# Scores of two heads as products of 64 rows in turns, in a fused attention and two feed-forward stages

## The chip, the cores and the metric

The kernel runs on one core of one Trainium2 chip. The metric is the device time of one execution in microseconds, as the median of several executions. TensorE multiplies and transposes, VectorE (DVE), ScalarE (ACT) and GpSimd (POOL) work element by element, SyncE (SP) issues the DMAs. Products land in PSUM, of which the kernel uses eight banks; everything else is kept in SBUF.

## What is computed

Three stages one after another, all in float32, for a batch of 4 sequences of 448 positions: a causal attention of 12 heads of width 64; a feed-forward of width 1024 with a convolution over three positions and a gate; and a mixture of 4 experts, each of which is a causal attention of one head of width 64, weighted by a gate that takes the best two of four.

```
scores = scale * np.matmul(q, k.transpose(0, 1, 3, 2))
scores = np.where(mask, -1000000000.0, scores)
attn = softmax(scores)
x = np.matmul(attn, v)
...
h = np.maximum(x @ w_in, 0.0)
conv_out = sum of conv_w[k] * h shifted by k - 1
x = h * sigmoid(conv_out) @ w_out
...
for e in range(E):
    q, k, v = x @ wq[e], x @ wk[e], x @ wv[e]
    a = causal softmax of scale * (q @ k.transpose(0, 2, 1))
    out += gate weight of e * (a @ v @ wo[e])
```

## The kernel before

**Planner.** The kernel does not issue its work as it is written. Each step is given to a planner (class `Plan`, `P.op`) with its cost on each engine that may do it, the buffers that it reads (`r`) and writes (`w`), and a function that issues it. `run` (L291) works out a rank for each step, lays the steps on the engines in simulated time (`schedule`, L330), moves the ranks by the table `SHIFTS` of seeded noise in given windows, and then issues all steps in order of their planned start. So the order on every queue, and which of ScalarE, VectorE and GpSimd does a conversion, follow from the cost figures and from `SHIFTS`; at run time each engine works through its own queue in that order and waits on semaphores. TensorE's steps are named "T", VectorE's "V", ScalarE's "A", GpSimd's "G", DMAs "D". A step is planned as one piece: nothing else is put between the instructions that its function issues.

**Split products.** Precision is kept by splitting a float32 operand into a high part, rounded to the type that TensorE takes in one pass (`high`, L595), and a low part, the difference (`low`, L606). A product a*b is summed in PSUM as high*high + low*high + high*low, three passes (`products`, L888). A head has only 64 rows to contract, half of TensorE's 128, so the scores (L615 to L688) use stacked operands: for one head, `qs` holds q's high part on the head's own 64 rows and q's low part on the other 64; `kh` holds k's high part on both halves; `kl` (tile `z`) holds k's low part on the own half and zeros on the other. Two products of 128 rows then make the three terms:

```
nc.tensor.matmul(bank(c), qs()[:, rows], kh()[:, kc(c)], start=True, stop=False)
nc.tensor.matmul(bank(c), qs()[:, rows], kl()[:, kc(c)], start=False, stop=True)
```

**Score blocks.** The 448 query positions are cut into four row blocks `c` (`Q0`, `QN`), whose causal widths are 64, 192, 320 and 448 columns. Blocks 3 and 0 of a head share the PSUM bank `sx`, blocks 2 and 1 the bank `sy`. For each block there are two products (L653, L654), a masked minimum that VectorE reads out of the bank (L660), and an exponential with its sum on ScalarE (L664). Then come reciprocals and a scaling of the weights (L674 to L688), transposes on TensorE (L691), the products with v (`weigh`, L741) and the splitting of the result (`gather`, L765). There is one `sx` and one `sy`, so the next head's blocks wait until VectorE has read the bank.

**Operands of the scores.** For 21 of the 24 attention pairs of heads `prepare` (L776) loads q and k of two heads as [128 rows, 2, 448], head 0 on rows 0 to 63 and head 1 on rows 64 to 127 (tile `full`), and makes the stacked operands: per head a conversion of 64 rows by 896 columns (q and k high), a copy of k high to the other half on ScalarE ("k again"), q low to the other half, and k low into `z`. The first three pairs (`WHOLE_QK`) skip the splitting: their scores are full float32 products of 128 rows with a block-diagonal k (L651). In the expert stage `project` (L1051) computes q and k of two experts at once into a bank `pf` and makes the same stacked operands per expert: two high parts of q and two of k on ScalarE, two low parts of q, two copies of k and the low parts of k on VectorE.

**Stages.** The attention of batch 0 runs first, beside the conversion of the feed-forward's weights; the attention of batch b + 1 is laid beside the feed-forward of batch b; the expert stage, with the projections of two batches ahead, follows from about 380 us on. In `full`, only one load of q and k (`raw`) is held at a time.

## Time and profile before

| what | us |
|---|---|
| median of 3 runs | 626.16 |
| lowest and highest run | 621.04, 626.28 |
| the profiled execution's own time | 625.61 |
| its span, first to last instruction | 623.8 |
| mean granted TensorE clock, share of full speed | 0.986 |

The profile is one execution, taken by the hardware profiler. Its views give busy time per engine, stretches of the span, groups of instructions by line and shape, the timeline, and the chain of work that ended last. PE is TensorE's products, PEld its weight loads, which run beside the products. Matmuls are pipelined and their ends are modelled: a product's own duration holds the time that it takes to pass through the array, so the distance between starts, not the duration, says what a product costs in a run of products. Idle time of an engine that is not the bottleneck costs nothing.

### The profile page before, as it was taken

How to read it: one execution, taken by the hardware profiler on the slowest of the kernel's cores; microseconds unless marked ns; L12 is line 12 of the kernel's file. 1: busy time of each engine (PE TensorE's matmuls, PEld its weight loads, DVE VectorE, ACT ScalarE, POOL GpSimd, SP SyncE). 2: the span in 40 equal slices, each digit the busy share in tenths (PEclk: the TensorE clock that was granted, in tenths of full speed). 3: DMA queues.
4: the chain of work that ended last, by engine and by line, in shares of the span. 5: the costliest groups of instructions: out<-in, count | busy, mean ns of one | idle time of the engine just before them, and what ended most of it. 6: DMA issues, size and time to landing. Idle time of an engine off the chain costs nothing.

```text
span 623.8 us, 10496 instructions
## 1 busy us (share of the span) xinstructions
PE 589.8 (95%) x3348; PEld 522.1 (84%) x3348; DVE 512.0 (82%) x1391; ACT 445.4 (71%) x1102; POOL 215.5 (35%) x241
## 2 busy tenths in 40 slices
PE   7999999989899999998999999979999899999997
PEld 3787788878788988887989987868999798999976
DVE  6999999998999979899987985982164979966982
ACT  5999798889779759999866994451142657745773
POOL 4765223545543016876201631641001202210320
PEclk9999999999799999998999999999999999999999
DMA  7645614374873065561007639616824040020123
GB/s 217 180 123 165 183 62 157 122 251 173 272 258 81 0 202 193 203 222 43 2 17 241 197 109 392 193 47 245 310 51 150 30 149 30 2 89 0 46 85 137
DMA packets 50455, 87.75 MB, mean 141 GB/s; under 512 B 21856, under 2 KB 31456, under 8 KB 50400
## 3 DMA queue, kind: packets, MB, share of 16 engines
q1 hardware_dynamic: 50400, 87.09, 42.9%
q8 instruction: 26, 0.43, 0.3%
q14 instruction: 29, 0.24, 0.1%
HBM read 64.26 MB, written 22.81 MB: 140 GB/s over the span
## 4 chain that ended last, share of the span: by engine, by line
PE 49%; DVE 25%; ACT 16%; issue 5%; DMA 3%; POOL 1%; SPq 1%; ACTq 0%; DVEq 0%; POOLq 0%
PE pf L896 30%; PE t L691 5%; DVE half L921 5%; DVE pair L607 4%; ACT e L664 4%; PE po L750 4%; DMA full<-in_qk 3%; ACT pair L599 3%; DVE a L607 3%; DVE e L660 3%; DVE z L607 2%; ACT e L680 2%; PE po L736 2%; ACT a L599 2%; PE sx L654 2%
## 5 line engine op out<-in xcount | busy, mean ns | idle before, releaser
L896 PE MATMUL pf<-pair,wbig 128*128 128x448 f32 x984 | 217.7, 370 | 5.4 <-ACT hp L910 4.1
L896 PEld LDWEIGHTS pf<-pair,wbig 128*128 128x128 f32 x984 | 180.6, 188 | 23.0 <-ACT hp L910 6.0
L664 ACT ACTIVATE e<-e,stat 128x448 f32<-128x448 f32 (+3 forms) x256 | 127.5, 500 | 19.5 <-DVE stat L660 18.5
L896 PE MATMUL pf<-pair,thou 128*128 128x448 f32 x576 | 133.5, 379 | 6.0 <-DVE pair L607 4.4
L896 PEld LDWEIGHTS pf<-pair,thou 128*128 128x128 f32 x576 | 108.8, 194 | 16.2 <-DVE pair L607 5.3
L691 PE MATMUL t<-ident,e 128*128 128x128 f32 x512 | 85.0, 280 | 3.5 <-DVE a L607 1.1
L607 DVE TENSOR_TENSOR a<-t,a 64x448 fp32r<-64x448 f32 (+1 forms) x96 | 75.5, 787 | 7.7 <-ACT a L599 5.9
L599 ACT ACTIVATE pair<-pf 128x448 fp32r<-128x448 f32 (+3 forms) x64 | 30.5, 492 | 60.3 <-PE pf L896 46.8
L691 PEld LDWEIGHTS t<-ident,e 128*128 128x128 f32 x512 | 61.6, 142 | 13.9 <-DVE a L607 4.7
L599 ACT ACTIVATE a<-t 64x448 fp32r<-64x448 f32 (+1 forms) x96 | 64.3, 673 | 8.8 <-PE t L691 6.0
L750 PE MATMUL po<-a,thou 128*128 128x384 f32 (+5 forms) x336 | 64.1, 312 | 2.4 <-DVE half L762 2.1
L683 POOL TENSOR_SCALAR e<-e,stat,coef 128x448 f32<-128x448 f32 (+3 forms) x37 | 21.3, 588 | 121.5 <-DVE coef L1165 63.5
L660 DVE CUSTOM_DVE_ANT_0 e<-sy,mask 128x192 f32<-128x192 f32 (+1 forms) x128 | 51.0, 416 | 10.5 <-PE sy L654 9.8
L607 DVE TENSOR_TENSOR pair<-pf,pair 128x448 fp32r<-128x448 f32 (+1 forms) x40 | 24.8, 621 | 35.6 <-ACT pair L599 35.1
L921 DVE SCALAR_TENSOR_TENSOR half<-hp,cws,half 128x448 f32<-128x448 f32 x64 | 49.9, 796 | 4.5 <-ACT half L916 4.0
L750 PEld LDWEIGHTS po<-a,thou 128*128 128x128 f32 (+1 forms) x336 | 47.6, 177 | 6.5 <-DVE half L762 3.4
L660 DVE CUSTOM_DVE_ANT_0 e<-sx,mask 128x448 f32<-128x448 f32 (+1 forms) x128 | 51.4, 414 | 1.9 <-PE sx L654 0.7
L607 POOL TENSOR_TENSOR pair<-half,pair 128x448 fp32r<-128x448 f32 x23 | 26.8, 1167 | 71.7 <-DVE pair L601 45.6
L680 ACT ACTIVATE e<-e,stat 128x192 f32<-128x192 f32 (+3 forms) x100 | 45.5, 501 | 5.0 <-DVE stat L676 4.7
L664 ACT ACTIVATION_READ_ACCUMULATOR e<-e,stat 128x1 f32 x256 | 48.3, 189 | 0.0
L599 ACT ACTIVATE pair<-full 64x448 fp32r<-64x448 f32 (+1 forms) x62 | 43.2, 696 | 6.3 <-DMA full<-in_qk 5.2
L607 POOL TENSOR_TENSOR thou<-half,thou 128x512 fp32r<-128x512 f32 x23 | 31.8, 1389 | 40.0 <-ACT thou L599 24.2
(116 smaller groups left out, 998.5 us busy)
## 6 DMA issues: line engine op xcount, KB each, us to landing
thou<-w_scratch SPq DMA_DIRECT2D x36, 512.0 KB, 5.0
x_scratch<-pair SPq DMA_DIRECT2D x24, 448.0 KB, 4.0
pair<-x_scratch SPq DMA_DIRECT2D x24, 448.0 KB, 5.4
full<-in_w_in SPq DMA_DIRECT2D x12, 512.0 KB, 4.0
full<-in_w_out SPq DMA_DIRECT2D x12, 512.0 KB, 4.0
w_scratch<-thou SPq DMA_DIRECT2D x12, 512.0 KB, 4.4
out<-half SPq DMA_DIRECT2D x24, 224.0 KB, 1.9
half<-in_vv SPq DMA_DIRECT2D x16, 256.0 KB, 5.0
```

What stands on the lines that cost most here:

```text
L599: nc.scalar.activation(dst(), src(), AF.Copy)
L607: return lambda e: engine(e).tensor_sub(dst(), src(), f32(h()))
L654: nc.tensor.matmul(bank(c), qs()[:, rows], kl()[:, kc(c)], start=False, stop=True)
L660: nc.vector.tensor_tensor_reduce(out=ec(c), in0=blocked(bank(c)), in1=blocked(m), scale=-0.125, scalar=3.0e38, op0=OP.add, op1=OP.min, acc ...
L664: nc.scalar.activation(ec(c), ec(c), AF.Exp, bias=st[:, 0, c:c + 1], scale=-1.0, accum_out=st[:, 1, c:c + 1])
L680: nc.scalar.activation(ec(c), ec(c), AF.Copy, scale=st[:, 3, c:c + 1])
L683: engine(en).tensor_scalar(ec(c), ec(c), st[:, 3, c:c + 1], gate, op0=OP.mult, op1=OP.mult)
L691: P.op({"T": TURN}, lambda _: nc.tensor.transpose(dst(), src(), ident), r=r, w=keys, m=m)
L736: lambda _, a=a, j=j, x=col + 64 * j - q, y=col + S - q: nc.tensor.matmul(ps[:, 64 * j:S], v(PLACE[j]), a[:, x:y], start=j == 0, stop=j == ...
L750: lambda _: nc.tensor.matmul(ps[:n, q:S], v(k, m), rhs(), start=start, stop=stop),
L896: nc.tensor.matmul(out_ap(), a(), b(), start=first, stop=end), r=r, w=[(ps, 0)])
L921: return lambda _: nc.vector.scalar_tensor_tensor(cv[:, :S], hp[:, i:S + i], cws[:, fc, i:i + 1], cv[:, :S], op0=OP.mult, op1=OP.add)
```

## The change

The stacked operands go. For a pair of heads there is one tile of high parts and one of low parts, q and k of head 0 on rows 0 to 63 and of head 1 on rows 64 to 127, as the load brings them. `prepare` needs one conversion of 128 rows by 896 columns and two subtractions of 128 rows by 448 columns; `project` one high and one low part of q for both experts, and per expert the high and low part of k. `scores` takes both heads of a pair. A row block has three products per head, q high with k high, q low with k high, q high with k low, each of 64 rows, and the two heads take turns product by product: head 0 on rows 0 to 63 into its bank `sx`, head 1 on rows 64 to 127 into its bank `sy`. Each head has one bank for all of its blocks: blocks 3 and 0 first, 2 and 1 after. The twelve products of two blocks are one step, which the planner counts as 3.6 (`SIDES`) times the time of one 128-row product of each width. The whole-precision scores of the first three pairs keep their form. The tiles `z` go, and there are 20 tiles `pair` in place of 18. Operands of the same values are multiplied; the rest of the computation is unchanged. The table `SHIFTS` is another, with 26 entries in place of 37, so the planner's order is new on all engines.

```diff
+SIDES = 3.6
...
 SHIFTS = (
-    (14931, 21, 61, 0.5), (51895, 149, 159, 2), (69609, 112, 152, 0.5), (19965, 135, 175, 0.5), (49972, 65, 75,
+    (50226, 530, 540, 1), (2079, 416, 436, 2), (83136, 282, 292, 1), (43264, 499, 539, 1), (58582, 209, 229, 1),
...
-      "qk high": ("AVG", "AVG"), "k again": "A", "q low": "VG", "k low": "VG", "v high": ("V", "AG")}
+      "qk high": ("AVG", "AVG"), "qk low": "VG", "v high": ("V", "AG")}
...
-    zs = tiles("z", 2, [128, 2, S], F32R)
-    for t in zs:
-        for o in range(2):
-            nc.gpsimd.memset(f32(t[HALF[1 - o], o]), 0.0)
...
-    zk = Kind(zs)
-    pairs = Kind(tiles("pair", 18, [128, 2, S], F32R))
+    pairs = Kind(tiles("pair", 20, [128, 2, S], F32R))
...
-    def scores(qs, kh, qk_r, kl, kl_r, j, e, turns=False):
-        sb = {3: P.buf("sx"), 2: P.buf("sy")}
-        sb[0], sb[1] = sb[3], sb[2]
-        st, o = P.buf("st"), j % 2
+    def scores(qk, j, e, turns=False):
+        whole = isinstance(qk, list)
+        sbs = [{3: P.buf("sx"), 2: P.buf("sy")} for _ in range(2)]
+        if not whole:
+            sbs = [{3: sbs[0][3], 2: sbs[1][3]}, {3: sbs[0][2], 2: sbs[1][2]}]
+        for sb in sbs:
+            sb[0], sb[1] = sb[3], sb[2]
+        sts = [P.buf("st") for _ in range(2)]
...
-        def bank(c):
-            return sb[c][:, COL[c]:COL[c] + Q0[c] + QN[c]]
...
+        def bank(o, c):
+            return sbs[o][c][:, COL[c]:COL[c] + Q0[c] + QN[c]]
+        def ec(o, c):
...
-        def kc(c):
+        def kc(o, c):
...
-        for c in ORDER:
-            w = Q0[c] + QN[c]
-            rows = slice(Q0[c], Q0[c] + 128)
-            if kl is None:
-                pe = 4 * w / 2400
-            else:
-                pe = product(w) + max(product(w), 0.107)
-            def mm(_, c=c, w=w, rows=rows):
-                if kl is None:
-                    nc.tensor.matmul(bank(c), qs()[:, rows], kh()[:, :w // 64], start=True, stop=True)
-                    return
-                nc.tensor.matmul(bank(c), qs()[:, rows], kh()[:, kc(c)], start=True, stop=False)
-                nc.tensor.matmul(bank(c), qs()[:, rows], kl()[:, kc(c)], start=False, stop=True)
-            P.op({"T": pe}, mm, r=qk_r + kl_r, w=[(sb[c], c)])
-            def mx(_, c=c, w=w):
+        def weight(o, c):
+            w, st, sb = Q0[c] + QN[c], sts[o], sbs[o]
+            def mx(_):
                 m = mask[:, 448 - w:448] if c and (o or turns) else mask[:, 320:320 + w]
-                nc.vector.tensor_tensor_reduce(out=ec(c), in0=blocked(bank(c)), in1=blocked(m), scale=-0.125, scalar=3.0e38,
+                nc.vector.tensor_tensor_reduce(out=ec(o, c), in0=blocked(bank(o, c)), in1=blocked(m), scale=-0.125, scalar=3.0e38,
                                                op0=OP.add, op1=OP.min, accum_out=st[:, 0, c:c + 1])
-            def ex(_, c=c):
-                nc.scalar.activation(ec(c), ec(c), AF.Exp, bias=st[:, 0, c:c + 1], scale=-1.0,
+            def ex(_):
+                nc.scalar.activation(ec(o, c), ec(o, c), AF.Exp, bias=st[:, 0, c:c + 1], scale=-1.0,
                                      accum_out=st[:, 1, c:c + 1])
             P.op({"V": on_vector(w)}, mx, r=[(sb[c], c)], w=[(e, (o, c)), (st, ("m", c))])
             P.op({"A": on_scalar(w) + 0.23}, ex, r=[(st, ("m", c))], w=[(e, (o, c)), (st, ("s", c))])
+        if whole:
+            for o, (qs, kh, r) in enumerate(qk):
+                for c in ORDER:
+                    w = Q0[c] + QN[c]
+                    P.op({"T": 4 * w / 2400}, lambda _, o=o, c=c, w=w, qs=qs, kh=kh: nc.tensor.matmul(
+                        bank(o, c), qs()[:, Q0[c]:Q0[c] + 128], kh()[:, :w // 64], start=True, stop=True), r=r, w=[(sbs[o][c], c)])
+                    weight(o, c)
+        else:
+            q, k, r = qk
+            for two in (ORDER[:2], ORDER[2:]):
+                def mm(_, two=two):
+                    for c in two:
+                        for i, (s, t) in enumerate(((0, 0), (1, 0), (0, 1))):
+                            for o, own in enumerate(HALF):
+                                nc.tensor.matmul(bank(o, c), q(s)[own, Q0[c]:Q0[c] + 128], k(t)[own, kc(o, c)], start=i == 0, stop=i == 2)
+                P.op({"T": sum(SIDES * max(product(Q0[c] + QN[c]), 0.107) for c in two)}, mm, r=r,
+                     w=[(sbs[o][c], c) for c in two for o in range(2)])
+                for c in two:
+                    for o in range(2):
+                        weight(o, c)
+        for o, st in enumerate(sts):
+            norms(j + o, st, o, ec, e)
+    def norms(j, st, o, ec, e):
...
-        raw, z = P.buf("raw"), P.buf("z")
-        sts = [P.buf("qks") for _ in range(2)]
+        raw, hi, lo = P.buf("raw"), P.buf("qks"), P.buf("qks")
...
         if turn:
-            P.op(dma_cost(229376, 1792), load(lambda: raw[:, :S], qk[p, :, 0]), w=[(raw, 0)], hold=[z] + sts)
+            P.op(dma_cost(229376, 1792), load(lambda: raw[:, :S], qk[p, :, 0]), w=[(raw, 0)], hold=[hi, lo])
...
         else:
-            P.op(dma_cost(458752), load(both, qk[p]), w=[(raw, i) for i in range(4)], hold=[z] + sts)
-        res, src = [], [(raw, i) for i in range(4)]
-        for o in range(2):
-            own, oth, st = HALF[o], HALF[1 - o], sts[o]
-            P.op(copy_cost(2 * S, ON["qk high"][ph]), high(lambda st=st, own=own: st[own], lambda own=own: both()[own]), r=src, w=[(st, 0)])
-            P.op(copy_cost(S, ON["k again"]), high(lambda st=st, oth=oth: st[oth, 1], lambda own=own: both()[own, 1]), r=src, w=[(st, 1)])
-            P.op(two_cost(S, ON["q low"]), low(lambda st=st, oth=oth: st[oth, 0], lambda own=own: both()[own, 0], lambda st=st, own=own: st[own, 0]),
-                 r=src + [(st, 0)], w=[(st, 2)])
-            P.op(two_cost(S, ON["k low"]), low(lambda own=own, o=o: z[own, o], lambda own=own: both()[own, 1], lambda st=st, own=own: st[own, 1]),
-                 r=src + [(st, 0)], w=[(z, o)])
-            res.append((lambda st=st: st[:, 0], lambda st=st: st[:, 1], [(st, i) for i in range(3)],
-                        lambda o=o: z[:, o], [(z, o)]))
-        return res
+            P.op(dma_cost(458752), load(both, qk[p]), w=[(raw, i) for i in range(4)], hold=[hi, lo])
+        src = [(raw, i) for i in range(4)]
+        P.op(copy_cost(2 * S, ON["qk high"][ph]), high(lambda: hi[:, :, :], both), r=src, w=[(hi, 0)])
+        for i in range(2):
+            P.op(two_cost(S, ON["qk low"]), low(lambda i=i: lo[:, i], lambda i=i: both()[:, i], lambda i=i: hi[:, i]), r=src + [(hi, 0)], w=[(lo, i)])
+        return lambda s: (hi, lo)[s][:, 0], lambda s: (hi, lo)[s][:, 1], [(hi, 0), (lo, 0), (lo, 1)]
...
-        return [(lambda: qw[:, :S], lambda o=o: kb[:, :, o], [(qw, 0), (kb, o)], None, []) for o in range(2)]
+        return [(lambda: qw[:, :S], lambda o=o: kb[:, :, o], [(qw, 0), (kb, o)]) for o in range(2)]
...
-            for o in range(2):
-                scores(*ops[o], 2 * p + o, e, whole)
+            scores(ops, 2 * p, e, whole)
...
-        heads = [(P.buf("q2"), P.buf("k2")) for _ in range(2)]
-        ops = {}
+        ops = []
...
-            (q, kh), kl = heads[pr], P.buf("kl2")
+            q, kt = P.buf("q2"), P.buf("k2")
...
-                for o in range(2):
-                    own, oth = HALF[o], HALF[1 - o]
-                    src = lambda ps=ps, own=own: ps[own, :S]
-                    if isk:
+                if isk:
+                    for o, own in enumerate(HALF):
                         more = 0.0 if o else 0.06
-                        P.op({"A": on_scalar(S) + more}, turn(high, o, lambda o=o, own=own, kh=kh: kh[own, o], src), r=[(ps, 0)], w=[(kh, (o, 0))])
-                        P.op(copy_cost(S, "V"), high(lambda o=o, oth=oth, kh=kh: kh[oth, o], lambda o=o, own=own, kh=kh: f32(kh[own, o])),
-                             r=[(kh, (o, 0))], w=[(kh, (o, 1))])
-                        P.op({"V": on_vector(S) + more}, turn(low, o, lambda o=o, own=own, kl=kl: kl[own, o], src, lambda o=o, own=own, kh=kh: kh[own, o]),
-                             r=[(ps, 0), (kh, (o, 0))], w=[(kl, (o, 0))])
-                        ops[2 * pr + o] = (lambda q=q, o=o: q[:, o], lambda kh=kh, o=o: kh[:, o],
-                                           [(q, (o, 0)), (q, (o, 1)), (kh, (o, 0)), (kh, (o, 1))],
-                                           lambda kl=kl, o=o: kl[:, o], [(kl, (o, 0))])
-                    else:
-                        P.op(psum_cost(S), high(lambda o=o, own=own, q=q: q[own, o], src), r=[(ps, 0)], w=[(q, (o, 0))])
-                        P.op({"V": on_vector(S)}, low(lambda o=o, oth=oth, q=q: q[oth, o], src, lambda o=o, own=own, q=q: q[own, o]),
-                             r=[(ps, 0), (q, (o, 0))], w=[(q, (o, 1))])
+                        src = lambda ps=ps, own=own: ps[own, :S]
+                        P.op({"A": on_scalar(S) + more}, turn(high, o, lambda own=own, kt=kt: kt[own, 0], src), r=[(ps, 0)], w=[(kt, (o, 0))])
+                        P.op({"V": on_vector(S) + more}, turn(low, o, lambda own=own, kt=kt: kt[own, 1], src, lambda own=own, kt=kt: kt[own, 0]),
+                             r=[(ps, 0), (kt, (o, 0))], w=[(kt, (o, 1))])
+                else:
+                    P.op(psum_cost(S), high(lambda q=q: q[:, 0], lambda ps=ps: ps[:, :S]), r=[(ps, 0)], w=[(q, 0)])
+                    P.op({"V": on_vector(S)}, low(lambda q=q: q[:, 1], lambda ps=ps: ps[:, :S], lambda q=q: q[:, 0]), r=[(ps, 0), (q, 0)], w=[(q, 1)])
+            ops.append((lambda s, q=q: q[:, s], lambda s, kt=kt: kt[:, s], [(q, 0), (q, 1)] + [(kt, (o, s)) for o in range(2) for s in range(2)]))
...
-            for o in range(2):
-                scores(*ops[2 * pr + o], B * H + b * E + 2 * pr + o, e)
+            scores(ops[pr], B * H + b * E + 2 * pr, e)
```

On TensorE, the scores of the first pair that is not in whole precision, before: pair_112 is the stacked operand of one head, z_98 its low part of k, block_105 and po_166 belong to the product of another pair's weights with v.

```order
L653 MATMUL sy_165<-pair_112 128x320
L654 MATMUL sy_165<-z_98,pair_112 128x320
L653 MATMUL sy_165<-pair_112 128x192
L654 MATMUL sy_165<-z_98,pair_112 128x192
L736 MATMUL po_166<-half_143,block_105 128x384
L736 MATMUL po_166<-half_143,block_105 128x128
L736 MATMUL po_166<-half_144,block_105 128x320
L653 MATMUL sx_164<-pair_112 128x64
L654 MATMUL sx_164<-z_98,pair_112 128x64
L653 MATMUL sx_164<-pair_112 128x448
L654 MATMUL sx_164<-z_98,pair_112 128x448
```

After, pair_106 holds the high parts and pair_107 the low parts of both heads; this is the first of the two steps of the pair, blocks of 448 and 64 columns.

```order
L669 MATMUL sx_160<-pair_106 128x448
L669 MATMUL sy_161<-pair_106 128x448
L669 MATMUL sx_160<-pair_106,pair_107 128x448
L669 MATMUL sy_161<-pair_106,pair_107 128x448
L669 MATMUL sx_160<-pair_107,pair_106 128x448
L669 MATMUL sy_161<-pair_107,pair_106 128x448
L669 MATMUL sx_160<-pair_106 128x64
L669 MATMUL sy_161<-pair_106 128x64
L669 MATMUL sx_160<-pair_106,pair_107 128x64
L669 MATMUL sy_161<-pair_106,pair_107 128x64
L669 MATMUL sx_160<-pair_107,pair_106 128x64
L669 MATMUL sy_161<-pair_107,pair_106 128x64
```

Eight products of a head came in pieces of two to four with other work between; now twelve products stand in one piece, and every second one goes to the other bank.

On VectorE, the operands of the first such pair before: full_136 is the load of q and k.

```order
L601 CAST pair_112<-full_136 64x896
L607 TENSOR_TENSOR z_98<-full_136,pair_112 64x448
L607 TENSOR_TENSOR pair_112<-full_136,pair_112 64x448
L607 TENSOR_TENSOR pair_113<-full_136,pair_113 64x448
L607 TENSOR_TENSOR z_98<-full_136,pair_113 64x448
L660 ISA e_159,stat_82<-sy_165,mask 128x5x64
```

After, the low parts of q and k of both heads, two instructions; the conversion to the high parts stands on GpSimd.

```order
L865 SCALAR_TENSOR_TENSOR half_140<-full_134,half_140 128x512
L694 TENSOR_SCALAR e_155<-e_155,stat_83 128x64
L694 TENSOR_SCALAR e_155<-e_155,stat_83 128x7x64
L600 TENSOR_TENSOR pair_107<-full_132,pair_106 128x448 x2
L644 ISA e_156,stat_84<-sy_161,mask 128x5x64
```

Five instructions of 64 rows became two of 128 rows, later in the queue; the three on ScalarE and none on GpSimd became one on GpSimd.

On VectorE, the operands of the first four experts before: pf_145 and pf_146 are the banks of the projections.

```order
L607 TENSOR_TENSOR pair_122<-pf_145,pair_122 64x448 x2
L601 CAST pair_119<-pair_119 64x448
L607 TENSOR_TENSOR z_99<-pf_146,pair_119 64x448
L607 TENSOR_TENSOR z_99<-pf_146,pair_119 64x384
L607 TENSOR_TENSOR z_99<-pf_146,pair_119 64x64
L601 CAST pair_119<-pair_119 64x448
L607 TENSOR_TENSOR pair_116<-pf_145,pair_116 64x448 x2
L601 CAST pair_113<-pair_113 64x448
L607 TENSOR_TENSOR z_98<-pf_146,pair_113 64x384
L607 TENSOR_TENSOR z_98<-pf_146,pair_113 64x64
L607 TENSOR_TENSOR z_98<-pf_146,pair_113 64x448
L601 CAST pair_113<-pair_113 64x448
```

After, in the same place:

```order
L600 TENSOR_TENSOR pair_111<-pf_141,pair_111 128x448
L600 TENSOR_TENSOR pair_117<-pf_142,pair_117 64x384
L600 TENSOR_TENSOR pair_117<-pf_142,pair_117 64x64
L600 TENSOR_TENSOR pair_117<-pf_142,pair_117 64x448
L600 TENSOR_TENSOR pair_115<-pf_141,pair_115 128x448
L600 TENSOR_TENSOR pair_106<-pf_142,pair_106 64x384
L600 TENSOR_TENSOR pair_106<-pf_142,pair_106 64x64
L600 TENSOR_TENSOR pair_106<-pf_142,pair_106 64x448
```

A subtraction of 128 rows stands for two of 64, and the copies of k within a tile (CAST pair<-pair) are gone; the low parts of k (448, or 384 and 64 columns) stay.

## Rows read from the trace of the kernel before

**Rows 1.** The page's table of engines: busy us, share of the span, instructions.
```profile
PE 589.8 (95%) x3348; PEld 522.1 (84%) x3348; DVE 512.0 (82%) x1391; ACT 445.4 (71%) x1102; POOL 215.5 (35%) x241
```

**Rows 2.** Stretches of the span: us; each engine's busy us and instructions; clock; DMA.
```profile
40.00:220.00 180.00, 169.67 (x913) 146.98 (x912) 172.27 (x433) 154.83 (x378) 71.15 (x70) 0.97 0.50 156
...
140.00:160.00 20.00, 16.79 (x90) 14.52 (x90) 18.31 (x49) 18.43 (x47) 11.31 (x13) 0.84 0.58 202
440.00:460.00 20.00, 20.00 (x101) 18.53 (x100) 5.74 (x11) 4.38 (x9) 0.00 (x0) 1.00 0.53 189
```

**Rows 3.** The page's chain of work that ended last, by engine.
```profile
PE 49%; DVE 25%; ACT 16%; issue 5%; DMA 3%; POOL 1%; SPq 1%; ACTq 0%; DVEq 0%; POOLq 0%
```

**Rows 4.** Timeline of TensorE, one head's score products: start, us, operation.
```profile
261.99 0.38 PE L653 MATMUL sy<-pair 128*128 128x320 f32 x1 [0.73 <-DVE stat L676]
262.21 0.31 PE L654 MATMUL sy<-z,pair 128*128 128x320 f32 x1
262.36 0.36 PE L653 MATMUL sx<-pair 128*128 128x448 f32 x1
262.56 0.37 PE L654 MATMUL sx<-z,pair 128*128 128x448 f32 x1
262.77 0.25 PE L653 MATMUL sy<-pair 128*128 128x192 f32 x1
262.86 0.28 PE L654 MATMUL sy<-z,pair 128*128 128x192 f32 x1
262.97 0.22 PE L653 MATMUL sx<-pair 128*128 128x64 f32 x1
263.02 0.28 PE L654 MATMUL sx<-z,pair 128*128 128x64 f32 x1
263.13 0.46 PE L896 MATMUL pf<-pair,thou 128*128 128x448 f32 x1
```

**Rows 5.** Timeline of TensorE's weight loads in the same stretch.
```profile
262.77 0.19 PEld L654 LDWEIGHTS sy<-z,pair 128*128 128x128 f32 x1
262.88 0.19 PEld L653 LDWEIGHTS sx<-pair 128*128 128x128 f32 x1
```

**Rows 6.** Groups by line and shape: count, busy us, mean ns of one, idle before.
```profile
L660 DVE CUSTOM_DVE_ANT_0 e<-sx,mask 128x448 f32<-128x448 f32 x64 | 39.4, 616 | 1.5 <-PE sx L654 0.7 <-PE sx L651 0.3
...
L599 ACT ACTIVATE pair<-full 64x448 fp32r<-64x448 f32 x42 | 24.2, 577 | 4.7 <-DMA full<-in_qk 3.9
...
L607 DVE TENSOR_TENSOR z<-full,pair 64x448 fp32r<-64x448 f32 x28 | 19.8, 707 | 0.4
...
L599 ACT ACTIVATE pair<-full 64x896 fp32r<-64x896 f32 x20 | 18.9, 947 | 1.6 <-DMA full<-in_qk 1.3
L607 DVE TENSOR_TENSOR pair<-full,pair 64x448 fp32r<-64x448 f32 x24 | 18.9, 788 | 0.7
...
L607 DVE TENSOR_TENSOR pair<-pf,pair 128x448 fp32r<-128x448 f32 x24 | 14.8, 621 | 24.8 <-ACT pair L599 24.6
...
L601 DVE CAST pair<-half 128x448 fp32r<-128x448 f32 x25 | 11.3, 456 | 0.3
...
L607 DVE TENSOR_TENSOR pair<-pf,pair 64x448 fp32r<-64x448 f32 x16 | 10.0, 622 | 10.8 <-ACT pair L599 10.6
...
L601 DVE CAST pair<-full 64x896 fp32r<-64x896 f32 x10 | 7.0, 699 | 4.5 <-DMA full<-in_qk 3.9 <-DMA x_scratch<-pair 0.5
...
L601 DVE CAST pair<-pair 64x448 fp32r<-64x448 f32 x16 | 6.5, 404 | 8.0 <-ACT pair L599 7.7
```

**Rows 7.** Timeline of TensorE, products into 64 columns between transposes.
```profile
252.41 0.42 PE L750 MATMUL po<-a,thou 128*64 128x128 f32 x2
252.68 0.49 PE L691 MATMUL t<-ident,e 128*128 128x128 f32 x3
```

More of the change, by code (lines that the diff above doesn't have):

```diff
@@ L579, in attention_moe_moe @@
             ("wbig0", big[0], 1), ("wbig1", big[1], 1), ("xs", pairs, 8), ("g", pairs, 8), ("qks", pairs, 4),
-            ("x2s", pairs, 2), ("x2", pairs, 12), ("y", pairs, 4), ("xm", pairs, 2), ("q2", pairs, 4), ("k2", pairs, 4), ("kl2", zk, 2),
+            ("x2s", pairs, 2), ("x2", pairs, 12), ("y", pairs, 4), ("xm", pairs, 2), ("q2", pairs, 4), ("k2", pairs, 4),
             ("vs", thou, 2), ("w2", thou, 4), ("w2b", thou, 6), ("vs2", thou, 6),
@@ L583, in attention_moe_moe @@
             ("hp", Kind(hps), 2), ("st", Kind(stats), 4),
-            ("e", Kind(tiles("e", 2, [128, 2048], F32)), 2), ("z", zk, 2), ("vb", bk, 2), ("kb", bk, 1), ("ab", half, 4),
+            ("e", Kind(tiles("e", 2, [128, 2048], F32)), 2), ("vb", bk, 2), ("kb", bk, 1), ("ab", half, 4),
             ("a0", Kind(tiles("a0", 2, [128, S], F32R)), 2), ("a1", Kind(tiles("a1", 1, [128, 2, 768], F32R)), 1),
@@ L679, in norm @@
                 if en == "A":
[L680 removed]
+                    nc.scalar.activation(ec(o, c), ec(o, c), AF.Copy, scale=st[:, 3, c:c + 1])
                 else:
                     gate = coef[:, b, c, x:x + 1] if moe else 1.0
[L683 removed]
+                    engine(en).tensor_scalar(ec(o, c), ec(o, c), st[:, 3, c:c + 1], gate, op0=OP.mult, op1=OP.mult)
             cost = scale_cost(Q0[c] + QN[c])
```

3 lines of the change are left out of this document (removed), and 12 rows, old and new, of the table SHIFTS.

## The prediction

> **What bounds the kernel now.** I read the table of engines first. TensorE is busy for 590 us of the 623.8 us span, VectorE for 512, ScalarE for 445 [rows 1]. A product counts as busy until its modelled end, so this share can't tell a full TensorE from one that waits between short products. The stretches tell more: from 440 to 460 us, in the projections of the last stage, VectorE has 5.7 us of work and TensorE is full; from 140 to 160 us, where the attention of one batch runs beside the feed-forward of another, VectorE and ScalarE are busy for over 18 us and TensorE falls to 16.8, in 90 products against 101, at a mean granted clock of 0.84; over the whole stretch from 40 to 220 us VectorE is at 172 of 180 us [rows 2]. The chain of work that ended last says the same: TensorE holds 49% of it, VectorE 25%, ScalarE 16% [rows 3]. No engine alone sets the end. TensorE is the first bound, and VectorE and ScalarE hold it up in the attention stages. The change touches all three, so there are two terms.
>
> **Term 1, TensorE.** Before, one head's scores are eight products: four row blocks of 448, 320, 192 and 64 columns, two products each. In one undisturbed run they reach from 261.99 to 263.13 us, 1.14 us [rows 4], and a pair of heads costs 2.28 us. 24 attention pairs less the three of the whole-precision path, and 8 expert pairs, make 29 pairs. Now a row block of a pair has six products of 64 rows, three for each half of the array, in turns: 24 a pair in place of 16, each with a load of its own weights.
>
> What one product costs is in the same rows, as the distance to the next start: 0.20 us for 448 columns, 0.15 for 320, and for the short ones about 0.11, since loads don't follow each other closer than that (262.77 to 262.88) [rows 4, 5]. Four row blocks make 0.57 us. No row of before shows two products on two halves, so I bound the pair:
> - both halves at once, loads too: 3 x 0.57 = 1.71 us, 0.57 less than now, x 29 = 16.5 us gained;
> - products at once, but loads taking turns at 0.11: 24 x 0.11 = 2.64 us, 0.36 more, x 29 = 10.4 us lost;
> - one product after another: 6 x 0.57 = 3.42 us, 1.14 more, x 29 = 33.1 us lost.
>
> I take the middle of the first two, 2.18 us, since the halves use different rows of the array, different operand rows and different banks, while nothing says whether two loads can be under way at once: 0.10 x 29, a gain of 3.0 us. The Trainium skill, "TensorE: Matmul & The Clock Gate", section "Part 3: Packing small matmuls — row/col tiling", says that products on different row groups run concurrently and gives 3.07 times for four of 32 rows; by it the first bound would hold, and the gain would be 16.5 us in place of 3.0. No run here shows it yet.
>
> The groups also change the shape of the array: each pair goes into the 64-row form twice and leaves it twice, 58 groups in all. A product of 448 columns takes 0.37 us and the next starts after 0.20 [rows 4], so letting the array run empty would cost 0.17 at each change, 0.34 a group, 19.7 us. The nearest row is of products into 64 columns between transposes: two of them, 128 and 256 columns, some 0.17 us of work by the 0.20 for 448, take from 252.41 to 252.68, so both changes together cost at most 0.10 us there [rows 7]. That is 0 to 5.8 us in 58 groups, and as part of the 0.10 is the transpose ahead still streaming, I take nothing. The Trainium skill, "TensorEngine Tiling (Array Packing)", section "Key Properties", speaks against the change here: changing the tiling mode drains TensorE. By that rule the 19.7 us would be due; the 64-column row does not agree, though it changes columns and not rows.
>
> A wait is added too. A group needs both banks, and the second group of a pair can't start until VectorE has read both banks of the first: at least the two reads of 448 columns, 2 x 0.62 us [rows 6]. Behind that wait stands all that the order has put after it on TensorE; the order puts feed-forward products or transposes in between, and where these run out the full 1.2 us x 29 = 36 us is the ceiling. I price it at nothing, since before, too, the next head waited for the bank, and the halving below covers a part.
>
> **Term 2, making the operands.** In attention, a pair took two conversions of 64 rows by 896 columns, two more copies of k, and four subtractions of 64 rows; now one conversion of 128 rows and two subtractions of 128 rows. An instruction's time goes by columns and not by rows: VectorE's subtraction of 448 columns takes 0.62 us from 64 rows or 128 [rows 6]. By line [rows 6]:
> - ScalarE: 18.9 + 24.2 = 43.1 us go, 11 conversions of 0.95 come back (count from the new order): 32.7 less.
> - VectorE: casts 7.0, subtractions 19.8 + 18.9, 45.7 together, go; 4 casts of 0.70 and 17 subtractions at the mean of 0.74 come back, 15.4: 30.3 less. In the experts, eight q subtractions and the 16 copies of k go: 8 x 0.62 + 6.5 = 11.5 less.
> - GpSimd loses some of the same work; at a third of the span busy it earns nothing.
>
> The planner spends part of this at once. The new order moves 21 more scalings of weights (86 against 65) and seven more casts of 448 columns to VectorE, 28 at about the cast's 0.46 us, 12.9 us, and four scalings, 2 us, to ScalarE. Net: VectorE 41.8 - 12.9 = 28.9 us less, ScalarE 30.7.
>
> How much of that is on the path? VectorE has 25% of the chain, 156 us out of its 512 busy, so 0.30 of a microsecond taken away is on it; ScalarE 16%, 100 of 445, or 0.22 [rows 1, 3]. That gives 8.7 + 6.8 = 15.5 us if nothing stands just behind. TensorE does stand behind, as its rows show outside of 140 to 160. I take half, 7.8 us, with 0 and 15.5 as bounds. What is late next is TensorE's own feed-forward products and ScalarE's exponentials, which are unchanged. DMA traffic is the same, and the two freed tiles join the pool of operand tiles, at no cost.
>
> **Sum.** 3.0 + 7.8 = 10.8 us less. The profiled execution took 625.6 us (span 623.8 and 1.8 around it), 0.6 under the median of 626.2 of the runs; from the median: 615 us.
>
> **Rivals.**
> - Everything works out: both halves at once and no engine just behind, 16.5 + 15.5 = 32 us, 594 us. For it: separate rows, operands and banks, and a full VectorE in the stretch. Against: TensorE is near its limit in most stretches, and the order is fitted to assumed costs.
> - Loads take turns: 10.4 lost, 7.8 gained, 629 us, no change. For it: in rows 5 loads never follow closer than 0.11. Against: those are loads for the same rows.
> - TensorE covers all: operands cost less but nothing is released, 3.0 gained, 623 us. For it: 95% busy. Against: VectorE's quarter of the chain.
> - The array empties at each change of shape: 19.7 - 10.8 = 8.9 lost, 635 us. Decides from 0.19 us a group up (10.8 / 58). Against: the 0.10 of the 64-column products.
> - The change doesn't do what it says, the halves don't run at once: 33.1 - 7.8 = 25 lost, 651 us, slower. The place is the 24 products of each pair, the price 1.14 us a pair, and it decides once a pair takes more than 2.28 + 7.8 / 29 = 2.55 us. For it: nothing in the trace shows concurrency.
>
> **How the numbers follow.** The forecast has 0.42 (its own range 607 to 620), everything works out 0.16, loads in turns 0.14, TensorE covers all 0.08, emptying 0.08, no concurrency 0.12. A measurement of this kernel tells about 1%, 6 us, from no change. Faster by more: 0.42 + 0.16 = 0.58; within: 0.14 + 0.08 = 0.22; slower: 0.20. The range leaves out the far case of no concurrency and about half of the best one: 597 to 638.
>
> **What would show it.** Right: starts of the two halves' products lie almost together; a pair's 24 products take about 2.2 us in two groups; the rows from the attention inputs shrink by 60% on ScalarE and VectorE; the stretch about 140 us holds more products. Wrong: starts 0.2 us apart in a group of 448 columns (no concurrency), 0.11 apart throughout (loads in turns), a gap at a group's ends (emptying), or VectorE's total down by 29 us with the same span (TensorE covers all).

## The result, and the profile after

The changed kernel takes 603.3 us, median of 4 runs (602.5 to 605.4), against 625.2 us for the one before (4 runs, 621.0 to 626.3): a ratio of 0.967, 95% interval 0.961 to 0.972. The gain is 21.9 us, where 10.8 were forecast; the direction was right, the size was not.

The profiled execution took 602.88 us, with a span of 601.1. First the page's table of engines and the chain of work that ended last:

```profile
span 601.1 us, 10782 instructions
PE 577.9 (96%) x3577; PEld 505.1 (84%) x3580; DVE 479.0 (80%) x1353; ACT 404.4 (67%) x1035; POOL 190.8 (32%) x207
...
PE 56%; DVE 7%; ACT 2%; DMA 1%; issue 1%; SPq 0%; POOL 0%; ACTq 0%
```

Beside [rows 1] VectorE has lost 33 us, ScalarE 41, GpSimd 25, TensorE 12. The chain can't be set beside [rows 3] as it is: its shares add up to two thirds, because it goes back only to 192.79 us, and the stretch in which VectorE is full lies mostly ahead of that. Its first piece, and the whole chain of the changed kernel in another order (without its table of shifts, see the experiments):

```profile
192.79 18.48 PE pf L896 x90
```

```profile
PE 64%; DVE 22%; DMA 6%; ACT 4%; issue 2%; SPq 1%; POOL 0%; DVEq 0%; ACTq 0%; POOLq 0%
```

And the kernel before without its table:

```profile
PE 40%; DVE 33%; ACT 14%; DMA 6%; issue 5%; POOL 1%; SPq 1%; ACTq 0%; DVEq 0%; POOLq 0%
```

Between these two, VectorE goes from 33% to 22%, ScalarE from 14% to 4% and TensorE from 40% to 64%. Stretches of the span, beside [rows 2]:

```profile
40.00:220.00 180.00, 173.40 (x1067) 149.12 (x1067) 165.16 (x435) 142.05 (x360) 74.50 (x73) 1.00 0.51 162
```

```profile
140.00:160.00 20.00, 19.63 (x136) 17.22 (x135) 19.62 (x58) 19.25 (x50) 13.10 (x15) 1.00 0.88 310
420.00:440.00 20.00, 20.00 (x100) 18.55 (x99) 3.81 (x7) 3.31 (x7) 0.00 (x0) 1.00 0.71 222
```

Where 90 products ran at a mean clock of 0.84, from 140 to 160 us, there are now 136 (smaller ones among them) at full clock; and VectorE is still at 165 of 180 us in the stretch from 40 to 220. A stretch of full TensorE (420 to 440) looks like the one of before (440 to 460). One group of 448 and 64 columns, and the ends of one of 320 and 192, in TensorE's timeline, beside [rows 4]:

```profile
241.66 0.41 PE L669 MATMUL sx<-pair 64*128 64x320 f32 x1
241.66 0.42 PE L669 MATMUL sy<-pair 64*128 64x320 f32 x1
241.91 0.31 PE L669 MATMUL sx<-pair,pair 64*128 64x320 f32 x1
241.92 0.31 PE L669 MATMUL sy<-pair,pair 64*128 64x320 f32 x1
...
242.43 0.27 PE L669 MATMUL sy<-pair,pair 64*128 64x192 f32 x1
242.63 0.66 PE L702 MATMUL t<-ident,e 128*128 128x128 f32 x4
...
244.84 0.47 PE L669 MATMUL sx<-pair 64*128 64x448 f32 x1
244.84 0.47 PE L669 MATMUL sy<-pair 64*128 64x448 f32 x1
245.15 0.35 PE L669 MATMUL sx<-pair,pair 64*128 64x448 f32 x1
245.15 0.36 PE L669 MATMUL sy<-pair,pair 64*128 64x448 f32 x1
245.35 0.36 PE L669 MATMUL sx<-pair,pair 64*128 64x448 f32 x1
245.36 0.36 PE L669 MATMUL sy<-pair,pair 64*128 64x448 f32 x1
245.55 0.19 PE L669 MATMUL sx<-pair 64*128 64x64 f32 x1
...
245.69 0.27 PE L669 MATMUL sx<-pair,pair 64*128 64x64 f32 x1
245.69 0.27 PE L669 MATMUL sy<-pair,pair 64*128 64x64 f32 x1
245.90 1.00 PE L761 MATMUL po<-a,thou 128*128 128x448 f32 x6
```

The two halves' products start together, at most 0.02 us apart, and the last two of three follow 0.20 us later for 448 columns and 0.15 for 320: what one product cost before. Only the first two of a group hold TensorE longer, 0.31 and 0.25 us. The loads of weights, beside [rows 5]:

```profile
242.32 0.19 PEld L669 LDWEIGHTS sx<-pair,pair 64*128 64x128 f32 x1
242.34 0.19 PEld L669 LDWEIGHTS sy<-pair,pair 64*128 64x128 f32 x1
242.63 0.42 PEld L702 LDWEIGHTS t<-ident,e 128*128 128x128 f32 x4
...
245.15 0.18 PEld L669 LDWEIGHTS sx<-pair,pair 64*128 64x128 f32 x1
245.16 0.18 PEld L669 LDWEIGHTS sy<-pair,pair 64*128 64x128 f32 x1
245.35 0.18 PEld L669 LDWEIGHTS sx<-pair 64*128 64x128 f32 x1
245.36 0.18 PEld L669 LDWEIGHTS sy<-pair 64*128 64x128 f32 x1
```

Two loads are under way at once, 0.01 us apart (245.15, 245.16), where loads for the same rows kept 0.11. But at the end of a group the next load (242.63) starts together with its product and not ahead of it. From its first product to the next other one a group takes 0.97 us for 320 and 192 columns and 1.06 for 448 and 64, 2.03 us a pair, which seems less than the 2.28 of before. But two delays lie outside of that count, the product ahead of a group and the first one behind it:

```profile
244.54 0.37 PE L896 MATMUL pf<-pair,thou 128*128 128x448 f32 x1
244.84 0.47 PE L669 MATMUL sx<-pair 64*128 64x448 f32 x1
```

```profile
245.90 0.47 PE L761 MATMUL po<-a,thou 128*128 128x448 f32 x1
```

```profile
246.21 0.45 PE L761 MATMUL po<-a,thou 128*128 128x256 f32 x2
```

After 448 columns the next product starts 0.30 us later in front of the group and 0.31 behind it, in place of 0.20. It is so throughout the trace: the medians are 0.297 us (27 groups behind a product of 448 columns) and 0.309 (31 groups ahead of one). With both delays counted (each product of 128 rows taken at its usual distance to the next), the medians of the 58 groups are 1.26 us for 448 and 64 columns and 1.15 for 320 and 192: 2.41 us a pair, 0.13 more than before. The operands, beside [rows 6] (count, busy us, mean ns):

```profile
L600 POOL TENSOR_TENSOR pair<-full,pair 128x448 fp32r<-128x448 f32 x25 | 30.5, 1229 | 8.0 <-ACT pair L592 4.4 <-DVE pair L594 2.7 <-DMA x_scratch<-pair 0.6
...
L600 DVE TENSOR_TENSOR pair<-pf,pair 128x448 fp32r<-128x448 f32 x32 | 19.7, 620 | 36.1 <-ACT pair L592 35.8
...
L600 DVE TENSOR_TENSOR pair<-full,pair 128x448 fp32r<-128x448 f32 x17 | 12.4, 736 | 0.1
...
L592 ACT ACTIVATE pair<-full 128x896 fp32r<-128x896 f32 x11 | 10.4, 946 | 1.0 <-DMA full<-in_qk 1.0
...
L594 DVE CAST pair<-full 128x896 fp32r<-128x896 f32 x4 | 2.5, 616 | 0.0
```

ScalarE's 43.1 us became 10.4, VectorE's 45.7 became 14.9 (12.4 + 2.5): the forecast's counts and durations hold.

### The profile page after: what moved, and what is told of

It is laid out like the page before. It is cut to its first block, busy times and chain, and to the rows that moved or that the text cites. A ratio compares the mean times of both kernels' runs of the same rounds, so it can differ in the third digit from the quotient of the medians.

```text
span 601.1 us, 10782 instructions
## 1 busy us (share of the span) xinstructions
PE 577.9 (96%) x3577; PEld 505.1 (84%) x3580; DVE 479.0 (80%) x1353; ACT 404.4 (67%) x1035; POOL 190.8 (32%) x207
## 4 chain that ended last, share of the span: by engine, by line
PE 56%; DVE 7%; ACT 2%; DMA 1%; issue 1%; SPq 0%; POOL 0%; ACTq 0%
PE pf L896 40%; PE po L761 5%; PE t L702 5%; PE sx L669 4%; DVE pair L600 1%; DVE half L921 1%; DMA thou<-w_scratch 1%; DVE a L600 1%; DVE e L644 1%; PE sy L669 1%; DVE half L773 1%; ACT pair L592 1%; ACT hp L910 0%; PE t L896 0%; DVE half L929 0%
## 5 line engine op out<-in xcount | busy, mean ns | idle before, releaser
L896 PEld LDWEIGHTS pf<-pair,thou 128*128 128x128 f32 x576 | 105.1, 188 | 15.7 <-DVE pair L600 5.4
L592 ACT ACTIVATE a<-t 64x448 fp32r<-64x448 f32 (+1 forms) x96 | 64.4, 674 | 16.5 <-PE t L702 11.2
L600 DVE TENSOR_TENSOR pair<-pf,pair 128x448 fp32r<-128x448 f32 (+3 forms) x56 | 30.1, 552 | 52.3 <-ACT pair L592 51.8
L592 ACT ACTIVATE pair<-pf 128x448 fp32r<-128x448 f32 (+3 forms) x56 | 26.3, 486 | 59.2 <-PE pf L896 57.7
L694 POOL TENSOR_SCALAR e<-e,stat,coef 128x192 f32<-128x192 f32 (+3 forms) x37 | 21.9, 605 | 131.3 <-DVE stat L687 57.7
L644 DVE CUSTOM_DVE_ANT_0 e<-sx,mask 128x64 f32<-128x64 f32 (+3 forms) x128 | 51.4, 416 | 6.1 <-PE sy L669 5.4
L644 DVE CUSTOM_DVE_ANT_0 e<-sy,mask 128x320 f32<-128x320 f32 (+3 forms) x128 | 50.7, 416 | 5.0 <-PE sy L669 3.4
L669 PE MATMUL sx<-pair,pair 64*128 64x448 f32 (+3 forms) x264 | 50.4, 306 | 0.1
L669 PE MATMUL sy<-pair,pair 64*128 64x448 f32 (+3 forms) x264 | 50.3, 306 | 0.0
L691 ACT ACTIVATE e<-e,stat 128x320 f32<-128x320 f32 (+3 forms) x104 | 46.8, 507 | 5.0 <-DVE stat L687 3.5
L669 PEld LDWEIGHTS sx<-pair,pair 64*128 64x128 f32 x264 | 41.5, 185 | 4.6 <-issue 2.2
```

The source lines that it names most:

```text
L592: nc.scalar.activation(dst(), src(), AF.Copy)
L600: return lambda e: engine(e).tensor_sub(dst(), src(), f32(h()))
L644: nc.vector.tensor_tensor_reduce(out=ec(o, c), in0=blocked(bank(o, c)), in1=blocked(m), scale=-0.125, scalar=3.0e38, op0=OP.add, op1=OP.mi ...
L669: nc.tensor.matmul(bank(o, c), q(s)[own, Q0[c]:Q0[c] + 128], k(t)[own, kc(o, c)], start=i == 0, stop=i == 2)
L691: nc.scalar.activation(ec(o, c), ec(o, c), AF.Copy, scale=st[:, 3, c:c + 1])
L694: engine(en).tensor_scalar(ec(o, c), ec(o, c), st[:, 3, c:c + 1], gate, op0=OP.mult, op1=OP.mult)
```

## Experiments

Three theories for the missing 11 us. One: the lighter operands are worth more than the half of the chain's share that the forecast gave them. Two: the forecast's terms hold and the new order, with its new table of shifts, brought the rest. Three: TensorE's shorter groups are all of it. Times are medians; each run stands beside runs of the kernel before on the same chip (623.6 to 625.3 us).

**Parts put back, in the changed kernel's own order.** In the first run every conversion of q and k and every subtraction is issued twice, and the copies of k are added inside the same steps; ScalarE's copies go to a spare tile. The planner does not know of it, so the order stays.

```diff
-        P.op(copy_cost(2 * S, ON["qk high"][ph]), high(lambda: hi[:, :, :], both), r=src, w=[(hi, 0)])
+        def twice(e):
+            for o in range(2):
+                step(e)
+                nc.scalar.activation(extra[:, :], both()[HALF[o], 1], AF.Copy)
...
+            P.op(two_cost(S, ON["qk low"]), lambda e, part=part: (part(e), part(e)), r=src + [(hi, 0)], w=[(lo, i)])
```

> The changed kernel in its own order, with the operand work of before put back in place: every conversion of q and k to high parts, and every subtraction, is issued twice, two copies of k per attention pair and per expert pair are added (some 40 us of work on VectorE and 37 on ScalarE). TensorE's work is as in the changed kernel. If the lighter operands are most of the gain (theory one): +12 to +18 us, about 618 us. If they are worth the 7.8 us of the forecast and the rest is the new order (theory two): about 611 us. If TensorE's shorter scores are all of it (theory three): within 3 us of the changed kernel, 603 to 606 us.

Measured: 647.5 us, 44 more than the changed kernel and 23 more than the one before. No theory said that. Putting the work back costs twice the whole gain, in an order that was made for short steps; which wait makes it so much, no run shows.

The second run has one product of each half once more in each group:

```diff
+                        if QN[c] + Q0[c] < 200:
+                            terms = ((0, 0),) + terms
```

> The changed kernel with one product of each half issued once more in each group of twelve (of the 64- or the 192-column block, its result overwritten), about 0.11 us a group, 6.4 us in 58 groups, so that a pair takes about the 2.28 us of before. If TensorE sets the end nearly everywhere now (theory three, and its share in theory one): +5 to +7 us, about 609 us. If TensorE has slack beside VectorE (theory two): +0 to +3 us, 603 to 606 us.

Measured: 609.3 us (604.5 to 610.4), 5.9 more for 6.8 us of products (a group takes 0.117 us longer in the trace, 58 groups). This is what was expected if TensorE sets the end nearly everywhere: time added on it comes through nearly whole in the changed kernel. It does not bear theory three out, since a pair costs TensorE 0.13 us more than before and not less.

Both together:

> Both additions together: operands as heavy as before and a pair's scores as long as before, in the order of the changed kernel. Theory one: the two terms are all, so 622 to 627 us, the time of before. Theory two: 613 to 616 us, and the 10 us that stay are the new order's. Theory three: 607 to 611 us.

Measured: 650.5 us, outside of every range again, and 3 above the heavy operands alone. With the operands heavy, TensorE's padding is about half hidden.

Then the products in another sequence, three of one half and then three of the other:

```diff
-                        for i, (s, t) in enumerate(((0, 0), (1, 0), (0, 1))):
-                            for o, own in enumerate(HALF):
+                        for o, own in enumerate(HALF):
+                            for i, (s, t) in enumerate(((0, 0), (1, 0), (0, 1))):
```

> The changed kernel with the three products of one half issued first, then the three of the other, in place of turns; the same products and loads. If halves run at once only when they take turns, a pair takes 6 x 0.57 = 3.4 us in place of 2.0, 1.4 x 29 = 40 us more on TensorE: 635 to 645 us. If the halves overlap in any sequence: 603 to 608 us. Each theory expects the same here; it sizes the rival in which the halves don't run at once.

Measured: 604.5 us, 1.2 more. TensorE's timeline in this run:

```profile
245.95 0.47 PE L669 MATMUL sx<-pair 64*128 64x448 f32 x1
245.96 0.47 PE L669 MATMUL sy<-pair 64*128 64x448 f32 x1
246.26 0.35 PE L669 MATMUL sx<-pair,pair 64*128 64x448 f32 x1
246.27 0.36 PE L669 MATMUL sy<-pair,pair 64*128 64x448 f32 x1
246.46 0.36 PE L669 MATMUL sx<-pair,pair 64*128 64x448 f32 x1
246.47 0.36 PE L669 MATMUL sy<-pair,pair 64*128 64x448 f32 x1
```

The halves run side by side although the queue holds three products for `sx` ahead of the three for `sy`. The rival in which they don't run at once is out, and the turns are not what makes them.

**Without the tables of shifts**, so that each variant gets an order planned for it.

```diff
-SHIFTS = ( ... )
+SHIFTS = ()
```

> The changed kernel with an empty table of shifts: the planner's own order, without the noise of the new table. If the new table is what made the gain larger than forecast (theory two): 612 to 618 us. If the table is worth little: 603 to 608 us.

> The kernel before with an empty table of shifts. What its table was worth: if as much as a table of this kind can bring, 630 to 640 us; if the tables bring nothing, 624 to 628 us. The distance from the changed kernel without a table is the change without its new order: 22 us or more if the tables play no part, about 11 us if theory two holds.

Measured: 611.1 us for the changed kernel, 7.8 above its time with the table; 639.9 us for the one before, 15.2 above the 624.7 of its runs there. The 611.1 lies between the two ranges, nearer to that of theory two, so the distance has to decide. The old table brought more than the new one. Theory two falls: without tables the change is worth more, 28.8 us, not less.

How far such orders scatter, with the start of TensorE in the plan 0.2 us earlier and nothing else changed:

```diff
-BEGIN = 6.5
+BEGIN = 6.3
```

> The kernel before without a table, planned with a start of TensorE at 6.3 in place of 6.5 us, which changes nothing but makes another order. It shows how far the time of an order without a table scatters. If orders scatter by under 3 us: 637 to 643 us, and the differences of the other runs without a table stand. If by 8 us or more, the split between scores and operands is not told by these runs.

> The same for the changed kernel: without a table, TensorE's start in the plan at 6.3 us. Under 3 us of scatter: 608 to 614 us.

Measured: 635.1 us before (4.8 lower than the other order), 611.9 us for the changed kernel (0.8 higher). The 4.8 lie between the two cases expected. Single differences of under 5 us between such runs say nothing.

**The heavy operands as planned steps.** The changed kernel's scores, and per head the conversions, copies and subtractions of before as steps of their own:

```diff
+        for own in HALF:
+            o = own.start // 64
+            P.op(copy_cost(2 * S, ON["qk high"][ph]), high(lambda own=own: hi[own], ...
+            P.op(copy_cost(S, "A"), lambda e, own=own: nc.scalar.activation(extra[:, :], both()[own, 1], AF.Copy), ...
+            for i in range(2):
+                P.op(two_cost(S, ON["qk low"]), low(lambda i=i, own=own: lo[own, i], ...
```

> The changed kernel's scores and banks, but the operands made by as many instructions as before (two conversions of 64 rows, two more copies of k on ScalarE, four subtractions of 64 rows in attention; in the experts two conversions and two subtractions of q and two copies of k), each a step of its own that the planner knows, and no table of shifts. Against the changed kernel without a table: +12 to +18 us if the lighter operands are most of the gain once the order is made for them (theory one), +6 to +9 us if half of the chain's share, as forecast; +35 us or more if the 44 us of the run with the work put back in a fixed order are the true price.

> The same with the heavier operands in the attention pairs alone, the experts as in the changed kernel, no table. Theory one expects nearly all of the difference to stay, since the attention stages have the full VectorE: within 4 us of the run with both. If the experts' waits for the projections' banks matter as much: half of the difference.

Measured: 623.9 us with both, 623.9 with the attention alone heavy: 12.8 above the changed kernel without a table, and no part of the experts can be made out.

> The run with the heavy operands and no table, with one product of each half issued once more in each group of twelve as in the padded run (result overwritten), which the planner knows (its factor at 4.0 for 3.6). A pair then costs TensorE about the 2.28 us of before and its operands what they cost before; what is left of the change is the form of the scores: one bank for each head, both heads in one step. If TensorE's shorter groups are all of the 16 us between this kernel and the one before without a table: 638 to 641 us. If they are worth their 0.22 x 29 = 6 us: 629 to 631 us, and some 10 us belong to the banks, the tiles or the order.

> The run with the heavy operands and no table, with 18 operand tiles in place of 20 and room for the operands of two expert pairs in place of four. If the larger pool of tiles is what makes the scores' part larger than TensorE's share: 630 to 636 us. If not: 621 to 627 us.

Measured: 635.6 us padded, 640.9 with less room. Both lie outside of the ranges expected, and both differences, 11.7 and 17, are above what either cause should give, so I took the two changes of room apart, with light operands and with heavy ones:

```diff
-    pairs = Kind(tiles("pair", 20, [128, 2, S], F32R))
+    pairs = Kind(tiles("pair", 18, [128, 2, S], F32R))
...
-("q2", pairs, 4), ("k2", pairs, 4)
+("q2", pairs, 2), ("k2", pairs, 2)
```

> The changed kernel without a table, with 18 operand tiles as before in place of 20. If the two freed tiles are a large part of the gain: 620 us or more, against 611 and 612. If their worth was within the scatter of orders: 608 to 616 us.

> The changed kernel without a table, 20 tiles, but room for the operands of two expert pairs in place of four, about what two tiles z allowed before. If this room is the cause: 620 us or more, and TensorE's gaps in the last stage. If not: 608 to 616 us.

> Heavy operands, no table, 18 tiles, room for four expert pairs. If the tiles are the cause of the 17 us between 623.9 and 640.9: 636 us or more. If the room for expert pairs is: 621 to 628 us.

> Heavy operands, no table, 20 tiles, room for two expert pairs. The other way round: 621 to 628 us if the tiles are the cause, 636 us or more if the room for expert pairs is.

Measured: 609.6 and 609.2 us light, 629.4 and 635.2 heavy. With light operands the room is worth nothing. With heavy ones each change costs something, but the expectation that one of the two carries the 17 us missed: these orders scatter more. Taken as orders of one kernel, the four light ones lie at 609.2 to 611.9, mean 610.5, and the four heavy ones at 623.9 to 640.9, mean 632.4. By these means the lighter operands are worth 21.9 us, which is the whole measured gain only by chance. The order of 640.9 has no light one with the same room; where the room is the same, the differences are 12.4, 19.8 and 26.0 us, mean 19.4. Each of the four heavy orders is slower than each light one by about 12 us or more, so that the operands count is shown, as theory one has it, and theory three falls; the size is not known better than 12 to 26 us. The heavy ones stand 5.1 us below the mean of the two orders of before without a table, 637.5. That would be the part of the scores, but heavy orders lie up to 17 us apart, so it is not told from nothing.

**Work or waiting.** Six more steps for each attention pair, two conversions, two copies and two subtractions of 64 rows by 448 columns out of a constant tile into spare ones, planned, with 18 operand tiles. In the first run nothing waits for them, in the second the scores do. The second run's edit (in the first, `Buf(ap=mask)` stands in place of `hi` in the third line, and the scores do not list `more`):

```diff
+        for i in range(2):
+            for n, (cost, fn) in enumerate(((copy_cost(S, ON["qk high"][ph]), move), (copy_cost(S, "A"), move), (two_cost(S, ON["qk low"]), less))):
+                more.append((hi, (2 + n, i)))
+                P.op(cost, fn, w=[more[-1]], after=[first])
...
+        return lambda s: (hi, lo)[s][:, 0], lambda s: (hi, lo)[s][:, 1], [(hi, 0), (lo, 0), (lo, 1)] + more
```

> The changed kernel without a table, 18 operand tiles, and for each of the 21 attention pairs six more steps of 64 rows by 448 columns that may start when the pair's high parts are there: two conversions, two copies on ScalarE, two subtractions, out of a constant tile into spare ones, which nothing waits for; the planner knows them. If the work itself fills the engines: 620 us or more, as with the heavy operands. If what counts is the chain of steps ahead of the scores, and idle time of the engines takes such work in: 609 to 614 us. The forecast's way of counting (a share of the chain for each us of an engine) gives some 8 to 11 us more: 618 to 622.

> The same six steps for each pair, the same work, but the pair's scores wait for them. If the chain ahead of the scores is what counts: 8 us or more above the loose run. If the work is: within 4 us of it.

Measured: 629.2 and 637.4 us against 609.6. The table of engines of the kernel without these steps:

```profile
PE 580.2 (96%) x3578; PEld 504.4 (83%) x3580; DVE 487.2 (80%) x1374; ACT 401.4 (66%) x1028; POOL 184.4 (30%) x194
```

and with them, nothing waiting:

```profile
PE 591.1 (94%) x3580; PEld 513.4 (82%) x3580; DVE 513.4 (82%) x1403; ACT 434.1 (69%) x1101; POOL 212.7 (34%) x218
```

VectorE has 26 us more, ScalarE 33, GpSimd 28, and the kernel takes 19.6 us more, though no step waits for that work. With the scores waiting, 8.2 more. These are single orders. The 19.6 us stand clear of the 2.7 us over which the light orders spread: work costs time though nothing waits for it, as it would if other steps queue behind it. The heavy operands with the same room took 629.4 us, no more than this run, though there the scores wait. The 8.2 us for the chain ahead of the scores meet the expectation just so, but heavy orders scatter by more, so this part is not shown.

## Why the prediction was right in direction and wrong in size

- **The halves, right in kind.** Of the bounds for a pair, 1.71, 2.64 and 3.42 us, "both halves at once, loads too" holds inside a group: loads start 0.01 us apart. I had put the loads halfway to taking turns. The Trainium skill, "TensorE: Matmul & The Clock Gate", section "Part 3: Packing small matmuls — row/col tiling", has products of different row groups concurrent, and the trace agrees: two products of 448 columns in the 0.20 us of one.
- **The change of shape, a step that failed.** "I take nothing" should have been about 0.35 us a group: 2.41 - 1.71 = 0.70 us a pair, 20.3 us in 58 groups. This is the 0.34 us a group, 19.7 us in all, that I had worked out for an array that runs empty and then set aside; the 64-column products did not stand for it. The Trainium skill, "TensorEngine Tiling (Array Packing)", section "Key Properties", says that a change of tiling mode drains TensorE; the trace agrees in that no load goes ahead across a change, and in the price. Whether the array is quite empty is not shown: the modelled end of the product ahead (244.54 + 0.37 = 244.91) lies behind the group's start at 244.84. With 16.5 - 20.3, TensorE's products cost some 4 us more than before, where 3.0 less were forecast. That the two errors of this term, the loads and the change of shape, partly cancel is luck.
- **Operands, the step that made the miss.** The work taken away was forecast about right (VectorE 28.9 us, ScalarE 30.7; measured over all 33 and 41). "I take half, 7.8 us, with 0 and 15.5 as bounds" was wrong: the lighter operands are worth 12 to 26 us, mean 19.4, in orders made for them. The loose run speaks against the halving: by the forecast's shares its extra work is 0.30 x 26 + 0.22 x 33 = 15 us, and 19.6 came. My reading, which no run shows by itself: a share of the chain counts one chain, and in a stretch where VectorE is at 172 of 180 us every other chain passes through the same queue. The steps between a pair's load and its scores, which the forecast did not price, may count beside it (8 us in the tight run, a single order).
- **What is left over.** Without tables the change is worth 26.0 us (637.5 to 611.5). With 19.4 for the operands and some 4 lost on TensorE's products, about 10 us have no cause of their own here; the scatter of the orders can hold most of it. One place where it can lie is TensorE's waiting: counted with the waits beside and between them, the scores hold TensorE for 89.7 us before and 73.6 after, and for 94.6 and 79.4 without tables. With the heavy operands as planned steps it is 77.9, so this goes with the form of the scores and not with the weight of the operands. Whether the waits went or moved to other products was not tried.
- **The planner's own move of work to VectorE** (12.9 us in the forecast) left the gain intact; no run tested it alone.
- **The order, not priced.** The old table was worth 12.3 us (637.5 to 625.2), the new one 8.2 (611.5, the mean of the two plain orders, to 603.3). The poorer table takes 4.1 us of the 26.0 back, which leaves the 21.9.
- **The bank wait**, priced at nothing: right as far as the trace shows. In front of the 58 groups TensorE loses 1.4 us in all beyond the delay of the change of shape, and between the groups shown, transposes and feed-forward products fill the time from 242.63 to 244.84.

## What to carry to other kernels

Where an engine is over 95% busy through a stage, price work taken off it by what queues for it and not by half of its share of one chain: add the same work where nothing waits for it, and the difference is its price. Whether the steps between a load and its first use count besides the busy time is worth runs in several orders. Two products of 64 rows in separate halves, operands and banks cost as much as one of 128 rows (0.20 us for 448 columns), but a change of shape has a price, 0.35 us here for going into the 64-row form and out again, so keep many of them together. Count a group from the product ahead of it to the second one behind it: from its first product to the next other one, this group looked cheaper than what it replaced.

## What the runs showed that I had not expected

The halves overlap without taking turns in the queue: three products in a row for one half and then three for the other start in pairs 0.01 us apart, and cost 1.2 us more in all, within the spread of the runs. And an order is worth as much as a change: the same work of the kernel before took 624.7, 635.1 and 639.9 us in three orders, and 44 us went into steps made longer in an order that was not planned for them, where orders planned for about the same work took 12 to 26.

The mean granted clock was 0.986 before and 1.00 after in the profiled executions, with 0.84 from 140 to 160 us before, part of the time at the lower of its two levels (1.2 GHz). It fell at 139.5 us, shortly after TensorE had waited 1.88 us for the low part of k, an operand that the change does away with in this form:

```profile
137.90 0.47 PE L654 MATMUL sx<-z,pair 128*128 128x448 f32 x1 [1.88 <-DVE z L607]
```

Over the runs on record, a run with a clock lower by 0.01 took about 4 us longer than others of the same kernel. Between the mean clocks of 0.989 before and 0.997 after that would be some 3 of the 21.9 us; whether the clock is the cause there or a sign of more waiting is not shown.
